# One transfer in place of four for the inverse of a unit, and one in place of three for the 80-row part of a stack

## The chip, the cores and the metric

The kernel runs on one core of one Trainium2 chip. The metric is device time in microseconds of one execution; the number that counts is the median of the runs.

## What is computed

The first part is a linear recurrence over 768 time steps for 4 batches of 8 heads (each state is 40 x 40):

```python
for t in range(S):
    y[:, :, t] = einsum('bhd,bhde->bhe', rt, state)
    Sa = einsum('bhde,bhe->bhd', state, at)
    state = state * wt[:, :, None, :] - einsum('bhd,bhe->bhde', Sa, bt) + einsum('bhd,bhe->bhde', vt, kt)
```

Its output, laid out as 3072 rows of 320, goes through a mixture of experts: noisy top-2 routing over 8 experts, `relu(x @ w1[e]) @ w2[e]` for the rows of each expert, weighted and summed.

## The kernel before

The recurrence is done in chunks of 64 time steps. Two pairs of batches (`p` = 0, 1) and 12 chunks give 24 units, numbered `n` = 0 to 23 in the order of their work. Four units (two chunks of both pairs) make a group `g` = 0 to 5. Within a unit the recurrence becomes matrix products with the inverse of a unit triangular matrix, which is built from 32 x 32 diagonal blocks: four blocks (`i` = 0 to 3) for each of 8 heads.

Preparation of a group, for each `p` (`prepA`, `scoresL`, `prepC`):

- VectorE takes running products of `w` (L495) and scales `b` (L518), `a` (L520) and `k` (L544) by them; ScalarE and VectorE split each into two half-precision parts, `pk` (L459, L460). `b` and `a` go to a buffer in HBM called `d_ab` (stores at L519 for `b`, L521 for `a`), `k` to `d_k` (L547). The input tiles `rawba` and `rawk` exist once, so the next load of each (L491, L538) waits until the split of the last one has read it.
- A stack `st_ab` of 120 rows is read back from `d_ab`: rows 40 to 119 with three transfers, one for each `gg` (L524), rows 0 to 39 with two, one for each of `a` and `b` (L525).
- TensorE multiplies `a` with `b` from the stack (`psc<-st_ab`), ScalarE copies the results to `lt` and `lo` (L556), and four transfers put the 32 x 32 blocks into `scr` in HBM (L558).
- `tsolve` loads `scr` as `X` with one matrix in each of 128 partitions (L563), masks it (L564), inverts by 30 steps of a multiply (L570) and an add (L571), and stores the result to `scr2` (L573). Groups 0 and 1 do this on VectorE, groups 2 to 5 on GpSimd (`TPOOL`).

A unit (`chain`, `outp`): `fetchA` loads `Vz`, `vu`, `st_k`, `RV` (L580, L581, L478, L585), `fetchB` loads the inverse `T` from `scr2` two units ahead, with four transfers of 32 partitions (L593). `apply` multiplies with `T` (`pQ<-w,T`), twice in a unit. The output row block is `xt` (L691), stored at L95, and routed a few units at a time.

All these transfers but GpSimd's own are issued from one queue, SyncE's (SP in the profile), which is in order: where one transfer waits for its data or its buffer, all behind it wait. A scheduler of the build sets the order on every engine, from priorities in the code (`high_priority`) and its own estimate of times; the estimate changes with the number of transfers, so the written order of the code doesn't fix the order of the program. Engines run their own instructions in order too. After the units, eight experts follow (`hidden` at L287, `output` at L309); their weights are loaded at L224, L225 and L229, those of the first expert while the last units run.

Of the kernel before, what the change touches and what calls it, by code (L numbers as in the profile page):

```python
# [8 lines left out]
F32 = mybir.dt.float32  # L9
# [354 lines left out]
NP,NG,CG,C=2,6,2,64  # L364
# [39 lines left out]
class Att:  # L404
# [81 lines left out]
    def prepA(s,p,g):  # L486
        nc=s.nc; FM=s.aps[0]; V=Behind(s.tc,nc.vector,s.tl) if g==1 else nc.vector
        sh=[120,NS,64]; W0=NS*65
        w=s.inp.tile([120,W0],F32,name="raww",bufs=2); nc.sync.dma_start(w,FM[p,g][:,:W0])
        ba=s.inp.tile([120,2*X],F32,name="rawba",bufs=BAB)  # L490
        for i in range(2): nc.sync.dma_start(ba[:,X*i:X*i+X],FM[p,g][:,W0+X*i:W0+X*i+X])  # L491
        b_,a_=ba[:,:X],ba[:,X:]
        Gx=s.tmp.tile([120,NS,65],F32,name="Gx")
        fl=lambda z: z.rearrange("p a b->p (a b)")
        V.tensor_tensor_scan(fl(Gx),w,fl(s.d1),0.0,op0=ALU.mult,op1=ALU.add)  # L495
        P=Gx[:,:,1:65]
        r0=w[:,:X].rearrange("p (a b)->p a b",a=NS)
        nc.scalar.activation(r0,P,AF.Ln)
        nc.scalar.activation(r0,r0,AF.Exp,scale=-1.0)
        NH=s.tmp.tile(sh,F32,name="NH",bufs=2)  # L500
        V.tensor_tensor(NH,P,r0,op=ALU.mult)
        nr=r0
        V.scalar_tensor_tensor(nr,NH,2.0,r0,op0=ALU.subtract,op1=ALU.mult)
        V.tensor_tensor(NH,nr,P[:,:,31:32].to_broadcast(sh),op=ALU.mult)
        NG_=s.late.tile(sh,F32,name="NG_",bufs=NGB)
        s.pl=(V if g in MG else nc.gpsimd).tensor_tensor(NG_,Gx[:,:,0:64],nr[:,:,31:32].to_broadcast(sh),op=ALU.mult)
        nge=s.tmp.tile([120,CG+1,3,2],F32,name=f"nge{p}",bufs=2)
        v4=lambda z: z.rearrange("p (a c b) t->p c a b t",a=3,c=CG)
        if g==0: V.memset(nge[:,0],0.0)
        else: V.tensor_copy(nge[:,0],s.nge[p][:,CG])  # L510
        V.tensor_tensor(nge[:,1:CG+1],v4(Gx)[:,:,:,:,64],v4(nr)[:,:,:,:,31],op=ALU.mult)
        s.nge[p]=nge
        gm=s.tmp.tile([120,2,3,CG],F32,name="gm")
        V.tensor_tensor(gm.rearrange("p b a c->p c a b"),nge[:,0:CG],v4(Gx)[:,:,:,:,32],op=ALU.mult)
        G={'p':p,'g':g,'NH':NH,'ng':NG_.rearrange("p (a c b) t->p a c (b t)",a=3,c=CG),'gm':gm}
        d=s.dr.tile([2,120,2,X],F16,name="d_ab",bufs=2)
        dv=d.rearrange("l p x n->p l x n")
        (V if g in MD else nc.gpsimd).tensor_tensor(b_,b_,fl(NH),op=ALU.mult)  # L518
        s.pack(b_,-SC,1,1,V=V,out=lambda pk: nc.sync.dma_start(dv[:,:,1],pk))  # L519
        (V if g in MD else nc.gpsimd).tensor_tensor(a_,a_,fl(NG_),op=ALU.mult)  # L520
        s.pack(a_,-SC,0,1,V=V,out=lambda pk: nc.sync.dma_start(dv[:,:,0],pk))  # L521
        st=s.sab[(2*g+p)%SAB].tile([120,18*K],F16,name="st_ab")
        sv=st.rearrange("p (g x n)->p g x n",g=3,x=2); dv=d.rearrange("l (e g) x n->(l e) g x n",g=3)
        for gg in range(3): nc.sync.dma_start(sv[40:120,gg],dv[:,gg])  # L524
        for x in range(2): s.sd0=nc.sync.dma_start(sv[0:40,:,x],dv[40*x:40*x+40,:,x])  # L525
        for i,z in enumerate('ab'): G[z]=[s.operand(st,2,i,CG,c) for c in range(CG)]
        pg=s.ps.tile([128,3,3*CG],F32,name="pg",tag="pp",bufs=s.PPB)
        for gg in range(3):
            for b in range(2):
                nc.tensor.matmul(pg[64*b:64*b+64,gg],s.selg[:,gg],gm[:,b].rearrange("p a c->p (a c)"),start=True,stop=True)  # L530
        gv=s.gam[p][:,:,g*CG:(g+1)*CG]
        V.tensor_copy(gv,pg.rearrange("p q (a c)->p (q a) c",a=3))
        return G
# [15 lines left out]
    def scoresL(s,G,gi,scr):  # L549

        nc=s.nc
        lt=s.tmp.tile([128,CG,8,32],F32,name="lt",bufs=LTB)
        lo=s.late.tile([128,CG,8,32],F32,name="lo",bufs=LOB)
        for c in range(CG):
            pp=s.score64(G['b'][c],G['a'][c],"pp",s.PPB)
            for z,t0 in ((lt,0),(lo,32)): nc.scalar.activation(z[:,c],pp[:,:,t0:t0+32],AF.Copy,scale=-(2.0**-18))  # L556
        for i in range(4):
            s.sl=s.nc.sync.dma_start(scr[gi,i].rearrange("c h (j t)->j (c h) t",j=32),(lt,lo)[i%2][32*i:32*i+32].rearrange("p c h t->p (c h) t"))  # L558
        G['lo']=lo
    def tsolve(s,scr,eng):  # L560
        nc=s.nc
        Xt=s.tmp.tile([128,32,32],F32,name="X",bufs=2)
        s.xd=s.nc.sync.dma_start(Xt.rearrange("p a b->p (a b)"),scr.rearrange("g i c h x->(g i c h) x"))  # L563
        eng.tensor_tensor(Xt,Xt,s.tri,op=ALU.mult)  # L564
        eng.memset(Xt.rearrange("p a b->p (a b)")[:,0:1024:33],1.0)
        T=s.tmp.tile([128,240],F32,name="Tt")
        for j in range(1,31):
            m=31-j
            t=T[:,:j*m].rearrange("p (k i)->p k i",i=m)
            eng.tensor_tensor(t,Xt[:,j:j+1,j+1:].to_broadcast([128,j,m]),Xt[:,0:j,j:j+1].to_broadcast([128,j,m]),op=ALU.mult)  # L570
            s.tl=eng.tensor_tensor(Xt[:,0:j,j+1:],Xt[:,0:j,j+1:],t,op=ALU.add)  # L571
        scr2=s.dr.tile([2,4,CG,8,32,32],F32,name="scr2")
        (nc.gpsimd if eng is nc.gpsimd else nc.sync).dma_start(scr2.rearrange("g i c h j x->(g i c h) (j x)"),Xt.rearrange("p j t->p (j t)"))  # L573
        return scr2

    def fetchA(s,G,cc,c,n):
# [12 lines left out]
        return o  # L589
    def fetchB(s,o,scr2,n):  # L590
        nc=s.nc; G,c=o['G'],o['c']; p=G['p']; T=s.Ts[n]=s.stk.tile([128,8,32],F32,name="T",bufs=TB)
        for i in range(4):
            s.nc.sync.dma_start(T[32*i:32*i+32],scr2[p,i,c].rearrange("h j x->j h x"))  # L593
    def warm(s,src,k):
        if not k: return
        for _ in range(k): s.nc.tensor.matmul(src,s.idh,s.dm[:,0:320],start=True,stop=True)
# [96 lines left out]
    def run(s,m,xo=None):  # L693
        nc=s.nc
        grp={}; scr={}; scr2={}; O={}
        N=NG*4
        def prepA(g,p):
            if p==0: grp[g]=[]; scr[g]=s.dr.tile([2,4,CG,8,1024],F32,name="scr")
            with s.tc.high_priority(offset=PA_):
                G=s.prepA(p,g); grp[g].append(G); s.scoresL(G,p,scr[g])  # L700
        def prepT(g):
# [3 lines left out]
        def idx(n): g,q=divmod(n,4); c,p=divmod(q,2); return g,c,p,g*CG+c  # L705
# [4 lines left out]
        def fB(n):  # L710
            if n<N: s.fetchB(O_(n),scr2[idx(n)[0]],n)
        after=s.tc.issue_after
        prepA(0,0); prepA(0,1); pl=s.pl.ins; prepT(0); xd,tl=s.xd.ins,s.tl.ins
        gate=(s.sd0,s.sl)
        s.prepC(grp[0][0],gate)
# [4 lines left out]
        with after(xd),(after(tl) if TG else ExitStack()):  # L720
            prepA(1,0); prepA(1,1); prepT(1)
# [3 lines left out]
        for n in range(N):  # L725
            g,c,p,cc=idx(n); ga,qa=divmod(n+LA,4); gc,qc=divmod(n+LC,4)
            if ga>1 and ga<NG and qa<2:
                with (after(s.sd0.ins) if n<=GA else ExitStack()): prepA(ga,qa)
                if qa: prepT(ga)
            if 0<gc<NG and qc<2:  # L730
                with (after(s.sd0.ins) if n<=GC else ExitStack()): prepC(gc,qc)
            with s.tc.high_priority(offset=PRIO):
                sD=s.chain(p,cc,O[n])
            fB(n+2)
            if n+1<N: s.pre(O[n+1])
            xt=s.wk.tile([128,360],F32,name="xt",bufs=2)
            s.outp(O[n],sD,xt); xt=xt[:,0:DM]
            if n+1<N: s.blocks(O[n+1])
            fA(n+2)
            if m is not None:  # L740
                m.drain(1); m.logits(2*cc+p,xt,s.ps,("pt","pp"),(s.PT,s.PPB))
                if ZN<=n<ZN+4:
                    with after(m.xw.ins): m.zero(n-ZN)
            else: nc.sync.dma_start(xo[p,cc],xt)
# [153 lines left out]
```

## Time and profile before

| | us |
|---|---|
| median of 3 runs (1033.17 to 1034.09) | 1033.28 |
| the profiled execution | 1035.52 |
| its span, first to last instruction | 1033.7 |
| busy TensorE, VectorE, ScalarE, GpSimd | 814.5, 554.3, 391.0, 321.1 |
| share of the chain that ended last: TensorE, VectorE, DMA, SP's queue | 53%, 21%, 14%, 3% |

The profile is of one execution, 2.2 us above the median. Busy times are shares of the span; the chain that ended last is followed back from the last instruction, at each step to what released it. A view by windows gives each engine's busy time in a stretch, the TensorE clock granted there (1.00 is 2.4 GHz, 0.50 is 1.2 GHz) and the mean busy share of the 16 DMA engines.

### The profile page before, as it was taken

What the parts mean: (1) busy time and instruction counts of PE and PEld (TensorE: products, weight loads), DVE (VectorE), ACT (ScalarE), POOL (GpSimd) and SP (SyncE); (2) the same over time, 40 slices, a digit from 0 to 9 for tenths busy, and PEclk for the clock granted to TensorE, in tenths of its full rate; (3) what the DMA queues carried; (4) which work ended last, traced back from release to release, by engine and by line L of the source; (5) the groups of instructions that cost most, each with busy time, mean ns of one, the idle gap of its engine ahead of it and who ended that gap; (6) DMA issues with size and microseconds to landing.
All of it is one profiled execution on the core that took longest, in us unless ns stands there. A gap on an engine that the chain in (4) does not pass through costs nothing.

```text
span 1033.7 us, 27409 instructions
## 1 busy us (share of the span) xinstructions
PE 814.5 (79%) x11706; PEld 712.2 (69%) x11706; DVE 554.3 (54%) x1198; ACT 391.0 (38%) x820; POOL 321.1 (31%) x456
## 2 busy tenths in 40 slices
PE   0114558669857876998896789999999999999994
PEld 0113446557746755877775668898989898989994
DVE  9268667944757666338554762643434444443420
ACT  2203443334633542454443432543434444443420
POOL 5000000393077039209401005316060606060312
PEclk9999986558967976998997699999999999999997
DMA  4785896593784684473486403516161616161302
GB/s 121 183 231 127 214 266 151 146 239 102 163 247 156 139 209 112 116 173 121 127 256 203 126 8 73 163 24 167 28 154 43 159 37 157 38 148 49 36 8 37
DMA packets 127111, 135.89 MB, mean 131 GB/s; under 512 B 59248, under 2 KB 106804, under 8 KB 126900
## 3 DMA queue, kind: packets, MB, share of 16 engines
q1 hardware_dynamic: 116292, 114.90, 41.5%
q0 software_dynamic: 10688, 19.14, 9.7%
q8 instruction: 94, 1.54, 0.6%
q14 instruction: 37, 0.30, 0.1%
HBM read 96.25 MB, written 41.03 MB: 133 GB/s over the span
## 4 chain that ended last, share of the span: by engine, by line
PE 53%; DVE 21%; DMA 14%; issue 4%; ACT 4%; SPq 3%; POOL 0%; POOLq 0%; DVEq 0%; ACTq 0%
PE po L309 17%; PE ph L287 15%; DMA rawk<-in_fm_dram 6%; PE psc L470 4%; PE pY L470 3%; DMA d_ab<-pk 2%; PE pW L470 2%; PE pQ L470 2%; PE pt L268 2%; DVE X L571 2%; DVE Tt L570 2%; DVE w2l L244 1%; DVE pk L460 1%; PE pst L470 1%; DVE ohB L162 1%
## 5 line engine op out<-in xcount | busy, mean ns | idle before, releaser
L311 POOL DMA_INDIRECT out_dram<-y,oi x56 | 92.3, 1648 | 236.9 <-ACT y L310 212.1
L290 DVE SCALAR_TENSOR_TENSOR hl<-ph,hh 128x256 fp32r<-128x256 f32 (+1 forms) x128 | 70.1, 554 | 120.5 <-ACT hh L288 111.3
L288 ACT ACTIVATE hh<-ph 128x320 fp32r<-128x320 f32 (+1 forms) x128 | 64.7, 518 | 147.6 <-PE ph L287 141.5
L564 POOL TENSOR_TENSOR X<-X,tri 128x1024 f32<-128x1024 f32 x4 | 9.0, 2242 | 309.2 <-DVE ak L606 179.3
L309 PE MATMUL po<-w2h,hh 128*128 128x320 f32 x384 | 75.4, 314 | 5.0 <-DVE y L304 3.9
L470 PE MATMUL psc<-RV,uT 128*64 128x128 f32 x384 | 63.0, 317 | 17.0 <-DVE P L680 15.1
L571 POOL TENSOR_TENSOR X<-X,Tt 128x30 f32<-128x30 f32 (+14 forms) x120 | 72.2, 602 | 8.7
L570 POOL TENSOR_TENSOR Tt<-X 128x30 f32<-128x30 f32 (+14 forms) x120 | 70.1, 584 | 8.4
L309 PE MATMUL po<-w2h,hl 128*128 128x320 f32 x384 | 70.8, 311 | 0.0
L287 PE MATMUL ph<-xh,w1h 128*128 128x512 f32 (+1 forms) x256 | 69.7, 355 | 1.0 <-DVE hl L290 1.0
L470 PEld LDWEIGHTS psc<-RV,uT 128*64 128x64 f32 x384 | 50.0, 160 | 27.6 <-DVE P L680 16.5
L287 PE MATMUL ph<-xh,w1l 128*128 128x512 f32 (+1 forms) x256 | 68.9, 350 | 0.0
L287 PE MATMUL ph<-xl,w1h 128*128 128x512 f32 (+1 forms) x256 | 68.6, 349 | 0.0
L252 POOL DMA_INDIRECT xr<-xd,gi x56 | 53.7, 959 | 47.6 <-issue 14.3
L309 PEld LDWEIGHTS po<-w2h,hh 128*128 128x128 f32 x384 | 61.0, 188 | 9.9 <-issue 5.0
L309 PE MATMUL po<-w2l,hh 128*128 128x320 f32 x384 | 65.7, 309 | 0.0
L470 PE MATMUL pQ<-w,T 32*32 32x40 f32 x2304 | 46.7, 224 | 23.7 <-DMA T<-scr 23.1
L680 DVE TENSOR_TENSOR P<-psc,mk 128x512 f32<-128x512 f32 x48 | 32.9, 686 | 59.3 <-PE psc L470 59.1
L470 PEld LDWEIGHTS pQ<-w,T 32*32 32x32 f32 x2304 | 39.6, 128 | 36.3 <-issue 32.1
L470 PE MATMUL psc<-RV 128*64 128x128 f32 x384 | 63.1, 317 | 0.0
L309 PEld LDWEIGHTS po<-w2h,hl 128*128 128x128 f32 x384 | 59.8, 188 | 0.5
L309 PEld LDWEIGHTS po<-w2l,hh 128*128 128x128 f32 x384 | 58.6, 188 | 0.1
(312 smaller groups left out, 1883.7 us busy)
## 6 DMA issues: line engine op xcount, KB each, us to landing
w2r<-in_w_dram SPq DMA_DIRECT2D x8, 1280.0 KB
RV<-in_rv_dram SPq DMA_DIRECT2D x48, 192.0 KB
rawba<-in_fm_dram SPq DMA_DIRECT2D x24, 360.0 KB
d_ab<-pk SPq DMA_DIRECT2D x24, 360.0 KB
st_ab<-d_ab SPq DMA_DIRECT2D x36, 240.0 KB
w1r<-in_w_dram SPq DMA_DIRECT2D x8, 1024.0 KB
raww<-in_fm_dram SPq DMA_DIRECT2D x12, 365.6 KB
st_ab<-d_ab SPq DMA_DIRECT2D x24, 180.0 KB
```

What stands on the lines that cost most here:

```text
L162: nc.vector.tensor_tensor(B[:,j],D[:,j].rearrange("p k (o m)->p k o m",o=1).to_broadcast([128,2,4,64]),vl[:,j].rearrange("p k (f o)->p k f ...
L252: k=t//128; nc.gpsimd.indirect_dma_start(out=X[:p,k if s.cap==CAP else 0],out_offset=None,in_=s.xd[int(w is not s.early[0])],in_offset=OFF ...
L268: for t,p in tiles(t0,n): nc.tensor.transpose(pt[:,t-t0:t-t0+p],x[:p,t//128,f0:f0+128],s.idm[:p,:p])
L287: for i,(a,b) in enumerate(mm): nc.tensor.matmul(ph[:,:n],a,b,start=i==0,stop=i==7)
L288: nc.scalar.activation(hh[:,f,:n],ph[:,:n],AF.Relu)
L290: if c.stop>c.start: nc.vector.scalar_tensor_tensor(o,ph[:,c],0.0,hh[:,f,c].bitcast(F32),op0=ALU.max,op1=ALU.subtract)
L309: s.lm=nc.tensor.matmul(po[:p],h[:,f,r],w[:,f],start=k==0,stop=k==23); k+=1
L311: st=nc.gpsimd.indirect_dma_start(out=s.out_d,out_offset=OFFS(ap=idx[:p,e,ii:ii+1],axis=0),in_=y[:p],in_offset=None,compute_op=ALU.add)
L470: def mm(s,*a,**k): return lambda: s.nc.tensor.matmul(*a,**k)
L570: eng.tensor_tensor(t,Xt[:,j:j+1,j+1:].to_broadcast([128,j,m]),Xt[:,0:j,j:j+1].to_broadcast([128,j,m]),op=ALU.mult)
L571: s.tl=eng.tensor_tensor(Xt[:,0:j,j+1:],Xt[:,0:j,j+1:],t,op=ALU.add)
L680: nc.vector.tensor_tensor(m,pp.rearrange("p i j t->p (i j) t"),s.mk.to_broadcast([128,8,64]),op=ALU.mult)
```

## The change

- `scr` and `scr2` keep their matrices in the order chunk, head, block in place of block, chunk, head (the block index `i` goes behind `c` and `h`). The stores of L558 write the same runs of 32 numbers to other places; the load and the store of `tsolve` stay one transfer each, with the matrices of the 128 partitions in the new order.
- With that order the rows `(i j)` of a unit's inverse lie at one stride, and `fetchB` loads all 128 partitions with one transfer in place of four. There are 24 units: 72 transfers fewer.
- The 80-row part of a stack is loaded with one transfer in place of three. There are 12 stacks: 24 transfers fewer.

No arithmetic changes. Lines after L593 are one lower in the changed kernel, and `T` is loaded at its L592.

```diff
-        for gg in range(3): nc.sync.dma_start(sv[40:120,gg],dv[:,gg])
+        nc.sync.dma_start(sv[40:120].rearrange("p g x n->p (g x n)"),dv.rearrange("p g x n->p (g x n)"))
...
-            s.sl=s.nc.sync.dma_start(scr[gi,i].rearrange("c h (j t)->j (c h) t",j=32),(lt,lo)[i%2][32*i:32*i+32].rearrange("p c h t->p (c h) t"))
+            s.sl=s.nc.sync.dma_start(scr[gi,:,:,i].rearrange("c h (j t)->j (c h) t",j=32),(lt,lo)[i%2][32*i:32*i+32].rearrange("p c h t->p (c h) t"))
...
-        s.xd=s.nc.sync.dma_start(Xt.rearrange("p a b->p (a b)"),scr.rearrange("g i c h x->(g i c h) x"))
+        s.xd=s.nc.sync.dma_start(Xt.rearrange("p a b->p (a b)"),scr.rearrange("g c h i x->(g c h i) x"))
...
-        scr2=s.dr.tile([2,4,CG,8,32,32],F32,name="scr2")
-        (nc.gpsimd if eng is nc.gpsimd else nc.sync).dma_start(scr2.rearrange("g i c h j x->(g i c h) (j x)"),Xt.rearrange("p j t->p (j t)"))
+        scr2=s.dr.tile([2,CG,8,4,32,32],F32,name="scr2")
+        (nc.gpsimd if eng is nc.gpsimd else nc.sync).dma_start(scr2.rearrange("g c h i j x->(g c h i) (j x)"),Xt.rearrange("p j t->p (j t)"))
...
-        for i in range(4):
-            s.nc.sync.dma_start(T[32*i:32*i+32],scr2[p,i,c].rearrange("h j x->j h x"))
+        s.nc.sync.dma_start(T,scr2[p,c].rearrange("h i j x->(i j) h x"))
...
-            if p==0: grp[g]=[]; scr[g]=s.dr.tile([2,4,CG,8,1024],F32,name="scr")
+            if p==0: grp[g]=[]; scr[g]=s.dr.tile([2,CG,8,4,1024],F32,name="scr")
```

The build's scheduler answers with another order of SP's queue and of the engines between the first unit and about the fourth; behind that the orders are nearly the same but for the merged transfers. Three places of SP's queue follow. The name of a tile is followed by the number of its buffer where the listing has one.

The first place is SP's queue where the stack of group 1, `p` = 1, is written and read (the stores of its `b` and its `a` half are L519 and L521; the 40-row reads at L525 need one half each). Before:

```order
L489 DMA raww<-in_fm_dram 120x780
L519 DMA d_ab<-pk 120x2x768
L521 DMA d_ab<-pk 120x2x768
L525 DMA st_ab<-d_ab 40x3x768
L491 DMA rawba<-in_fm_dram 120x768 x2
L524 DMA st_ab<-d_ab 80x1536 x3
L525 DMA st_ab<-d_ab 40x3x768
L547 DMA d_k<-pk 120x4x384
```

And in the changed kernel:

```order
L489 DMA raww<-in_fm_dram 120x780
L519 DMA d_ab<-pk 120x2x768
L525 DMA st_ab<-d_ab 40x3x768
L521 DMA d_ab<-pk 120x2x768
L491 DMA rawba<-in_fm_dram 120x768
L558 DMA scr<-lt 32x16x32
L558 DMA scr<-lo 32x16x32
L558 DMA scr<-lt 32x16x32
L524 DMA st_ab<-d_ab 80x4608
L525 DMA st_ab<-d_ab 40x3x768
L558 DMA scr<-lo 32x16x32
L547 DMA d_k<-pk 120x4x384
```

The store of the `a` half (L521) now stands behind the first 40-row read (L525), which waits for the `b` half to have landed, and three block stores of `p` = 0 stand ahead of the 80-row read.

The second place is SP's queue where the stack of group 2, `p` = 1, is read, the `k` of group 2 is stored (L547) and the next `k` is loaded (L538). Before:

```order
L524 DMA st_ab<-d_ab 80x1536 x3
L558 DMA scr<-lt 32x16x32
L585 DMA RV_175<-in_rv_dram 48x1024 x2
L558 DMA scr<-lo 32x16x32
L558 DMA scr<-lt 32x16x32
L558 DMA scr<-lo 32x16x32
L525 DMA st_ab<-d_ab 40x3x768
L547 DMA d_k<-pk 120x4x384
L538 DMA rawk<-in_fm_dram 120x768
```

And in the changed kernel:

```order
L524 DMA st_ab<-d_ab 80x4608
L585 DMA RV_175<-in_rv_dram 48x1024 x2
L525 DMA st_ab<-d_ab 40x3x768
L547 DMA d_k<-pk 120x4x384
L538 DMA rawk<-in_fm_dram 120x768
L519 DMA d_ab<-pk 120x2x768
L558 DMA scr<-lt 32x16x32
L558 DMA scr<-lo 32x16x32
L558 DMA scr<-lt 32x16x32
L558 DMA scr<-lo 32x16x32
```

The store and the load of `k` now stand ahead of the four block stores.

The third place is SP's queue behind the end of group 1's `tsolve`, where the inverses of units 4 to 7 are loaded. Before:

```order
L573 DMA scr_782<-X 128x1024
L489 DMA raww<-in_fm_dram 120x780
L95 DMA xd_839<-xt 128x320
L593 DMA T<-scr_782 32x8x32 x12
L580 DMA Vz_172<-in_vt_dram 64x320 x2
L547 DMA d_k<-pk 120x4x384
L593 DMA T<-scr_782 32x8x32 x4
L521 DMA d_ab<-pk 120x2x768
L491 DMA rawba<-in_fm_dram 120x768 x2
L538 DMA rawk<-in_fm_dram 120x768
```

And in the changed kernel, from the second pair of inverses on:

```order
L592 DMA T<-scr_768 128x8x32 x2
L581 DMA vu<-in_vt_dram 64x2x320
L558 DMA scr<-lt 32x16x32
L558 DMA scr<-lo 32x16x32
L558 DMA scr<-lt 32x16x32
L558 DMA scr<-lo 32x16x32
L580 DMA Vz_172<-in_vt_dram 64x320 x2
L563 DMA X<-scr 128x1024
L521 DMA d_ab<-pk 120x2x768
L491 DMA rawba<-in_fm_dram 120x768 x2
L547 DMA d_k<-pk 120x4x384
L538 DMA rawk<-in_fm_dram 120x768
```

The load of `k` (L538) now follows its store (L547) at once; no load of an inverse stands between them or ahead of `rawba`.

## Rows read from the trace of the kernel before

**Rows 1.** Windows by stage: units 0 to 3, the other units, the experts.
```profile
core 0: us, PE busy (x) PEld busy (x) DVE busy (x) ACT busy (x) POOL busy (x), PEclk, DMA share, GB/s
85.00:235.00 150.00, 95.44 (x1792) 79.99 (x1793) 108.52 (x192) 55.28 (x114) 35.62 (x47) 0.76 0.76 195
235.00:602.00 367.00, 300.36 (x7257) 248.16 (x7257) 216.65 (x507) 156.78 (x377) 127.65 (x236) 0.84 0.59 158
602.00:1033.70 431.70, 409.78 (x2488) 376.52 (x2486) 174.79 (x378) 163.65 (x305) 142.59 (x111) 0.99 0.35 80
```
**Rows 2.** The chain that ended last, 200 to 240: start, us, what.
```profile
209.74 8.32 DMA rawk<-in_fm_dram
...
218.12 7.05 DMA d_ab<-pk
...
227.50 5.14 DMA rawk<-in_fm_dram
```
**Rows 3.** VectorE's timeline: start, us, what, [idle before it, and its releaser].
```profile
149.24 1.23 DVE L564 TENSOR_TENSOR X<-X,tri 128x1024 f32<-128x1024 f32 x1 [1.82 <-DMA X<-scr]
...
172.36 1.02 DVE L544 TENSOR_TENSOR rawk<-rawk,NH 120x384 f32<-120x384 f32 x2 [6.45 <-DMA rawk<-in_fm_dram]
...
201.77 1.04 DVE L460 SCALAR_TENSOR_TENSOR pk<-rawk,pk 120x768 f16<-120x768 f32 x1
...
213.03 1.06 DVE L518 TENSOR_TENSOR rawba<-rawba,NH 120x768 f32<-120x768 f32 x1 [5.52 <-DMA rawba<-in_fm_dram]
...
218.08 1.43 DVE L544 TENSOR_TENSOR rawk<-rawk,NH 120x384 f32<-120x384 f32 x2 [1.21 <-DMA rawk<-in_fm_dram]
```
**Rows 4.** Line L593, the loads of `T`: nanoseconds min/median/max of an issue.
```profile
L593 SPq DMA_DIRECT2D T<-scr x96: 308/448/1803, 85.5 to 520.6; - x96
```
**Rows 5.** Windows: unit 0's start, the stretch after it, the first expert's weights.
```profile
85.00:95.00 10.00, 4.99 (x132) 4.27 (x134) 8.70 (x13) 3.51 (x6) 0.00 (x0) 1.00 0.42 77
95.00:165.00 70.00, 42.77 (x816) 35.91 (x810) 51.28 (x88) 30.67 (x61) 0.00 (x0) 0.90 0.92 235
520.00:560.00 40.00, 32.65 (x721) 25.74 (x707) 24.11 (x86) 13.86 (x37) 5.11 (x9) 0.85 0.88 256
```
**Rows 6.** SP's timeline at the third place: start, us, what.
```profile
196.94 5.75 SPq L593 DMA_DIRECT2D T<-scr  x12
...
204.02 0.54 SPq L547 DMA_DIRECT2D d_k<-pk  x1
204.61 3.08 SPq L593 DMA_DIRECT2D T<-scr  x4
...
209.74 0.48 SPq L538 DMA_DIRECT2D rawk<-in_fm_dram  x1
```
**Rows 7.** SP's timeline at the second place.
```profile
158.88 1.28 SPq L585 DMA_DIRECT2D RV<-in_rv_dram  x2
...
164.76 0.84 SPq L547 DMA_DIRECT2D d_k<-pk  x1
```
**Rows 8.** SP's timeline at the first place.
```profile
108.51 0.33 SPq L521 DMA_DIRECT2D d_ab<-pk  x1
112.43 0.78 SPq L525 DMA_DIRECT2D st_ab<-d_ab  x1
...
114.31 1.27 SPq L524 DMA_DIRECT2D st_ab<-d_ab  x3
```
**Rows 9.** SP's timeline at the loads for units 20 to 23.
```profile
507.10 4.61 SPq L593 DMA_DIRECT2D T<-scr  x8
511.81 2.07 SPq L580 DMA_DIRECT2D Vz<-in_vt_dram  x2
```
**Rows 10.** TensorE's timeline: scores of group 1; unit 20's first use of `st_k`.
```profile
124.77 0.64 PE L470 MATMUL psc<-st_ab 120*64 120x64 f16 x16 [4.38 <-DMA RV<-in_rv_dram]
...
526.89 0.43 PE L470 MATMUL psc<-st_ab,st_k 120*64 120x64 f16 x16
```

## The prediction

> **What bounds the kernel now.** I read the windows by stage first. The experts (the last 432 us) keep TensorE busy for 410 of 432 us at the full clock [rows 1], and the change touches nothing there. Units 4 to 23 take 367 us with TensorE busy for 300. The weak stretch is 85 to 235, units 0 to 3: TensorE is busy for 95 of 150 us at a granted clock of 0.76, VectorE for 109 [rows 1]. Then the chain of waits. In that stretch it runs through transfers that feed the preparation of the next groups: a load of `rawk` of 8.32 us, a store of `d_ab` of 7.05, the next `rawk` of 5.14 [rows 2]. Last VectorE's timeline: it is in order, carries both the preparation and the units, and stands still for 6.45 us at 172.36 and 5.52 us at 213.03 because a loaded input has not landed [rows 3]. TensorE's next matmuls wait behind it. So what counts is when SP's queue issues `rawk` and `rawba`, and the loads of `T` are worth something only where they stand ahead of those.
>
> The profiled execution took 1035.5 us, 2.2 us above the median. The sum is made against it and the same difference taken from the median.
>
> **The change part by part.** 96 issues go. One load of `T` takes 0.448 us to issue [rows 4]. A load of 128 partitions isn't in the trace: its issue lies between one of the shortest, 0.308, and four medians, 1.79. I take 0.45, because the queue's other issues stand near that whatever their shape: 0.54 for `d_k`, 0.48 for `rawk` [rows 6]. Then 72 loads of `T` and 24 of stacks are 43 us of SP's queue, but nearly all of it lies beside other work. The bytes and the short runs of `T` stay as they are, so its time on the DMA engines stays. The moves inside `scr` and `scr2` change only addresses: nothing, covered by the same transfers as before; if the new strides cost the block stores something, it would show as a later `X`.
>
> *Units 0 to 3's inverses (85 to 93).* Sixteen issues become four. VectorE is busy for 8.70 of the 10 us [rows 5], so what SP issues behind them isn't wanted sooner, and unit 0 needs all four parts either way. Nothing; the cover is VectorE's work, and without it the gain would be at most the 12 issues, 5.4 us.
>
> *Third place, units 4 to 7's inverses.* Before, VectorE finishes the split of `k` at 202.81 [rows 3], `d_k` is issued at 204.02 and over at 204.56, and then four loads of `T` (3.08 us), the store of `a` and two loads of `rawba` stand ahead of `rawk`, issued at 209.74 [rows 6]. In the new order `rawba` comes ahead of `d_k` and `rawk` right behind it. The earlier twelve loads of `T` shrink from 5.75 us to under 2, so `rawba` finds the queue free. `rawk` can go at 204.6: 5.1 us sooner. VectorE's waits that follow, 5.52 us for `rawba` and 1.21 for `rawk` [rows 3], are all of this kind, and the store and the next `rawk` of the chain [rows 2] follow from them. Bounds: nothing, if the transfer lands no sooner, and 6.7 us, both waits. I take 5.1, near the upper end, because the chain passes through just these issues. Late next is the split of `a` and `b` on ScalarE and VectorE.
>
> *Second place.* Before, the second `d_k` of group 2 is issued at 164.76, 4.6 us behind the end of `RV` (158.88 + 1.28 = 160.16) [rows 7]; between them stand three block stores that wait for ScalarE, and one stack read. In the new order only the stack read, 0.78 us as at 112.43 [rows 8], remains: `d_k` and `rawk` go 3.8 us sooner. VectorE waits 6.45 us for that `rawk` in the middle of `tsolve`, and 1.82 us at its start for `X` [rows 3], which moves ahead of three stack reads too. Bounds: nothing, and 8.3 us with both waits gone. I take 3.8, what the issue gains. What moves back, the four block stores, only has to reach GpSimd's `tsolve` of group 2, whose inverse isn't used before unit 8. From 95 to 165 the DMA engines are busy to 0.92 [rows 5], so there is little room for more.
>
> *First place.* The store of the `a` half waits for the `b` half to land: it moves from 108.51 to behind 112.43 + 0.78 = 113.21, 4.7 us later [rows 8]. The stack read at 114.31 waits for it; the read itself shrinks from 1.27 us to about 0.45, so the stack is some 3.9 us later. TensorE already waits 4.38 us for it at 124.77 [rows 10]. I count nothing, because the scores behind it are copied by ScalarE ahead of a split that stood in their way before, so `X` isn't later for it; if that cover is gone, 3.9 us (rival B).
>
> *Weights of the first expert.* They move ahead of unit 20's `st_k`, `RV` and unit 23's `T`. With three loads of `T` and two of `Vz` behind 507.10 [rows 9], the weights are issued from about 507.1 + 3 x 0.45 + 2.07 = 510.5. They are 2.9 MB by the shapes in the code; at the 256 GB/s of 520 to 560 [rows 5] they take 11.3 us, to 521.8. Unit 20's `st_k` is first used at 526.89 [rows 10]: 5 us of cover, so nothing; at 180 GB/s they would take 16 us and end there, and each us more would cost one.
>
> Sum: 5.1 + 3.8 = 8.9 us. The profiled execution would take 1035.5 - 8.9 = 1026.6, the median **1033.3 - 8.9 = 1024.4 us**.
>
> **The rivals.** The bound of a measurement here is about 0.2%, 2 us, so 1031.2 to 1035.4 is no change.
>
> A. *The DMA engines are the bound, not the queue: no change.* For it: a share of 0.92 from 95 to 165 [rows 5], with the same bytes to move. An issue that goes sooner then only waits in another place, `rawk` lands at 172 as before, and what is won at 204 is lost in the same way. Against it: at 85 to 95 the share is 0.42 [rows 5], and the load at 209.74 follows SP's issue at once. It gives 1033.3. The Trainium skill, DMA: Bandwidth & Descriptors, in "Issuing engines are not separate DMA queues", says that what is saved on a sequencer's issue time is usually small relative to the transfer itself; by that rule the sum would be near nothing. The trace agrees for most of the 96 issues, and not for those on the chain [rows 6].
>
> B. *The `a` half's store is caught behind a wait: slower.* The stack of group 1, `p` = 1, is 3.9 us later, TensorE stands at its scores in order with unit 1's second half behind them, `X` and VectorE's `tsolve` follow, and the full DMA engines take away the gains. It decides if the scores start later than 124.77 + 2, and `X` is masked later than 149.24. 1033.3 + 3.9 = 1037.2 us.
>
> C. *The merge doesn't do what it says:* the new strides might split the 128-partition load so that it fills one queue for four issues, 1.79 us. Then the third place would keep 3 x (0.448) of its 5.1 and the gain would be 7.6: still faster, at 1025.7.
>
> **How the numbers follow.** The forecast with C, faster by over 0.2%: 0.63. A: 0.16. B, and with it orders that the scheduler made worse where I haven't looked: 0.21. The lower end takes both upper bounds, 6.7 + 8.3 = 15.0, and 2 us more for a clock in units 0 to 3 that rises as waits go (0.76 now, 0.84 later [rows 1]): 1016. The upper end is B: 1037.5. Beyond lie fewer than 2 in 10.
>
> **What would show it.** In the profile after: 24 loads of `T` in L592 with an issue near 0.45 us; `rawk` issued under 1 us behind its `d_k` after VectorE's `tsolve`; VectorE's wait for `rawk` inside `tsolve` down from 6.45 us by about 4, and for `rawba` behind it near nothing; the window of units 0 to 3 about 9 us shorter, the experts' window unchanged. I am wrong if `rawk` lands as late as before although issued sooner (A), if the scores of group 1 start at 127 or later and `X` behind them (B), or if units 19 to 21 stand waiting for `st_k`.

## The result and the profile after

| | before | after |
|---|---|---|
| median of 4 runs each, one chip (us) | 1033.55 (1033.17 to 1034.09) | 1043.17 (1041.18 to 1047.09) |
| ratio, 95% interval | | 1.0103 [1.0067, 1.0139] |
| profiled execution / its span (us) | 1035.52 / 1033.7 | 1041.5 / 1039.8 |

The change makes the kernel 1% slower. I had forecast 1024.4, faster, with an upper end of 1037.5: the sign was wrong.

The windows by stage after the change, to be held against [rows 1, 5] (same columns):

```profile
core 0: us, PE busy (x) PEld busy (x) DVE busy (x) ACT busy (x) POOL busy (x), PEclk, DMA share, GB/s
85.00:95.00 10.00, 4.58 (x144) 4.20 (x144) 8.28 (x16) 4.56 (x7) 0.00 (x0) 1.00 0.60 118
85.00:235.00 150.00, 92.54 (x1873) 77.35 (x1873) 105.96 (x195) 56.03 (x116) 24.28 (x37) 0.80 0.77 196
```

VectorE is busy for 106 of the 150 us where it was busy for 109, and TensorE for 93 instead of 95: the weak stretch is as weak as before. The issue of the merged load went as assumed; this is its line (ns min/median/max), against [rows 4]:

```profile
L592 SPq DMA_DIRECT2D T<-scr x24: 383/474/2312, 86.2 to 517.3; - x24
```

SP's queue at the second place, against [rows 7] (start, us, what):

```profile
157.54 1.46 SPq L585 DMA_DIRECT2D RV<-in_rv_dram  x2
159.05 0.81 SPq L525 DMA_DIRECT2D st_ab<-d_ab  x1
159.90 0.51 SPq L547 DMA_DIRECT2D d_k<-pk  x1
160.46 0.47 SPq L538 DMA_DIRECT2D rawk<-in_fm_dram  x1
```

`d_k` goes at 159.90 in place of 164.76, 4.9 us sooner; I had counted 3.8. At the third place, against [rows 6]:

```profile
196.10 2.81 SPq L581 DMA_DIRECT2D vu<-in_vt_dram  x1
199.00 0.55 SPq L558 DMA_DIRECT2D scr<-lt  x1
...
202.71 0.35 SPq L563 DMA_DIRECT2D X<-scr  x1
203.15 0.39 SPq L489 DMA_DIRECT2D raww<-in_fm_dram  x1
203.59 0.38 SPq L95 DMA_DIRECT2D xd<-xt  x1
204.03 0.43 SPq L521 DMA_DIRECT2D d_ab<-pk  x1
204.50 1.75 SPq L491 DMA_DIRECT2D rawba<-in_fm_dram  x2
206.35 1.01 SPq L547 DMA_DIRECT2D d_k<-pk  x1
207.40 0.63 SPq L538 DMA_DIRECT2D rawk<-in_fm_dram  x1
```

`rawk` stands directly behind `d_k`, as the listing said, but goes at 207.40, 2.3 us sooner than 209.74 and not 5.1. `rawba` didn't find the queue free. From 196.10 on SP issues, with no pause above 0.3 us, what the new order puts ahead of it: a load of `vu` whose issue alone lasts 2.81 us (why was not followed), four block stores, `Vz`, `X`, `raww`, an `xd` store and the store of `a` (the listing of the third place lacks `raww` and `xd`). VectorE's split of `a` had ended at 202.39, 1.6 us before its store was issued, so the queue and not the split set the time of `rawba`. VectorE's own timeline has changed too (idle before, and its releaser, in brackets), against [rows 3]:

```profile
169.46 1.03 DVE L544 TENSOR_TENSOR rawk<-rawk,NH 120x384 f32<-120x384 f32 x2 [3.22 <-DMA rawk<-in_fm_dram]
172.04 0.48 DVE L690 TENSOR_TENSOR xt<-pY,xt 128x320 f32<-128x320 f32 x1
...
190.46 0.69 DVE L679 TENSOR_TENSOR P<-psc,mk 128x512 f32<-128x512 f32 x1 [1.93 <-PE psc L470]
...
194.61 0.69 DVE L605 TENSOR_TENSOR ak<-psc,mk 128x512 f32<-128x512 f32 x1 [1.69 <-PE psc L470]
197.23 0.96 DVE L506 TENSOR_TENSOR NG__2455<-Gx,raww 120x768 f32<-120x768 f32 x1 [1.92 <-PE pgm L471]
198.10 0.48 DVE L690 TENSOR_TENSOR xt<-pY,xt 128x320 f32<-128x320 f32 x1
...
202.78 0.95 DVE L460 SCALAR_TENSOR_TENSOR pk<-rawk,pk 120x768 f16<-120x768 f32 x1
...
212.78 0.96 DVE L518 TENSOR_TENSOR rawba<-rawba,NH 120x768 f32<-120x768 f32 x1 [4.91 <-DMA rawba<-in_fm_dram]
...
216.71 1.71 DVE L544 TENSOR_TENSOR rawk<-rawk,NH 120x384 f32<-120x384 f32 x2 [2.68 <-DMA rawk<-in_fm_dram]
```

And the end of unit 1 on VectorE before, which the prediction never looked at:

```profile
159.80 0.48 DVE L691 TENSOR_TENSOR xt<-pY,xt 128x320 f32<-128x320 f32 x1
```

The last step of unit 1 (`xt`) has moved from 159.80 to 172.04. The scheduler has put pieces of group 1's `tsolve` ahead of it on VectorE: 25 of its 60 steps in place of 9. With `tsolve` used up earlier (its store goes at 188.55, before at 193.81), VectorE has nothing to fill the gaps of units 2 and 3, and waits for TensorE at 190.46, 194.61 and 197.23. The split of `k`, which ended at 202.81 before, now starts at 202.78, behind unit 2's `xt`. The wait for `rawk` inside `tsolve` fell from 6.45 to 3.22 us. But up to the end of unit 3 VectorE's waits for `rawba` and `rawk` add to 19.5 us after and 17.6 before, and its waits for TensorE to 5.5 and 0.5: nothing was won in sum.

Where the time goes over all units is best read on one chip: three profiled executions there, the end of `xt` of a unit by VectorE's timeline (start plus duration), in us. The third kernel, explained below, merges `T` alone and keeps the order of before.

| end of unit | 1 | 3 | 7 | 18 | 19 | 21 | 23 | span |
|---|---|---|---|---|---|---|---|---|
| before (f1) | 159.7 | 226.4 | 306.6 | 512.2 | 526.4 | 575.3 | 603.2 | 1028.4 |
| after (f2) | 171.9 | 226.3 | 308.3 | 510.4 | 530.7 | 570.2 | 608.0 | 1034.6 |
| `T` merged, order of before (f3) | 159.1 | 220.6 | 298.7 | 506.9 | 521.2 | 564.8 | 592.6 | 1018.2 |

After the change, unit 3 ends when it did before; unit 7 is 1.7 us late; unit 19 loses 6 us, which come back by unit 21; units 22 and 23 take 37.8 us in place of 27.9. The experts take 425.2 us before and 426.6 after. On most chips executions of one kernel scatter by over 1%, so single profiles show places, and the ratios below show what a place costs.

### The profile page after: what moved, and what is told of

Its sections match the earlier page's. It is cut to its first block, busy times and chain, and to the rows that moved or that the text cites. A ratio compares the mean times of both kernels' runs of the same rounds, so it can differ in the third digit from the quotient of the medians.

```text
span 1039.8 us, 27317 instructions
## 1 busy us (share of the span) xinstructions
PE 814.2 (78%) x11706; PEld 713.9 (69%) x11706; DVE 554.7 (53%) x1198; ACT 391.4 (38%) x820; POOL 320.3 (31%) x456
## 4 chain that ended last, share of the span: by engine, by line
PE 59%; DVE 16%; DMA 14%; issue 4%; ACT 3%; SPq 3%; POOL 0%; POOLq 0%; DVEq 0%; ACTq 0%
PE ph L287 18%; PE po L309 16%; DMA rawk<-in_fm_dram 6%; PE psc L470 4%; PE pY L470 4%; PE pQ L470 2%; DMA d_ab<-pk 2%; PE pW L470 2%; PE pt L268 2%; DMA rawba<-in_fm_dram 2%; DVE X L571 1%; DVE Tt L570 1%; PE pu L471 1%; PE pS L470 1%; PE pst L470 1%
## 5 line engine op out<-in xcount | busy, mean ns | idle before, releaser
L470 PE MATMUL psc<-RV,uT 128*64 128x128 f32 x384 | 65.9, 327 | 30.3 <-DVE P L679 26.2
L470 PE MATMUL psc<-RV 128*64 128x128 f32 x384 | 66.0, 327 | 0.0
```

What stands on the lines that cost most here:

```text
L470: def mm(s,*a,**k): return lambda: s.nc.tensor.matmul(*a,**k)
```

## The experiments

The theory: merging `T` gains about what I forecast, but the changed number of transfers made the build's scheduler draw another order for all engines, and this order costs more than that. The rivals: the merged transfers themselves cost time (they land later, or delay others); the new addresses in `scr` and `scr2` cost; or the cost lies at one place, such as the first expert's weights.

The two orders differ a good deal. With the loads of `T` and of a stack counted as one each, 125 of 441 places on SP, 235 of 1175 on VectorE, 102 of 821 on ScalarE and 1062 of 8243 on TensorE hold another instruction; GpSimd's are the same. Most lie between 85 and 240 us; of VectorE's, 63 lie between 510 and 600, none in the experts. The order behind the fourth unit is thus less alike than the section on the change has it. To hold an order fixed, most kernels below add this to the end of the build: for each engine a chain of order-only edges, no wait and no work, after a table of the wanted order.

```diff
+def pin(nc,tc,table):
...
+        for a,b in zip(run,run[1:]):
+            tc.add_manual_dep(b,a.name,mybir.DependencyInfo(mybir.DependencyClass.NoSync,mybir.DependencyReason.DATA),reason="pin")
...
         build(nc, tc, aps, out)
+        pin(nc, tc, TABLE)
```

What differs from kernel to kernel is then the loads and the table; orders in pieces are cut by the time at which an instruction stands in the profile of before. Ratios are to the kernel before on the same chip, with 95% intervals. No run holds a kernel to its own order alone; the nearest is g3 below, held to before's order and at 1.0026.

**The order against the merges.** e1: the changed kernel, table of before's order. e2: the kernel before with its seven loads, table of after's order.

```diff
 e1: the changed kernel
+        pin(nc, tc, TABLE)
 e2: the kernel before
+        pin(nc, tc, TABLE)
```

> The changed transfers (one load of T, one stack load) with every engine's instructions pinned to the order of the kernel before. Theory O, the order: what was lost came with the order that the build's scheduler made of the new transfer count, so here it is gone: 1029 to 1034 us, with unit 7, unit 19 and units 22 to 23 as long as before (28.8, 14.3 and 27.8 us). Theory X, the transfers: a merged load lands later (T 3.65 us in the middle against 2.48 for a quarter, the stack part 7.41 against 5.92), and what waits for it starts later whatever the order: 1041 us or more.

> The reverse: the kernel before, with its four loads of T and three stack loads, pinned on every engine to the order of the changed kernel. Theory O: as slow as the changed kernel or slower, since 96 issues come back into the same order: 1041 to 1050 us. Theory X: the transfers are the old ones, so 1031 to 1035 us.

e1 measured 0.9913 [0.9879, 0.9948], e2 1.0125 [1.0072, 1.0179]. With the order held, both merges together are faster; with the old loads, the new order alone is slower. That is the theory's sign on both sides, and it rules out that the merged transfers are what costs.

**Which stretch of the order.** e3: both merges, after's order to 510 us and before's behind; e4 the reverse.

```diff
 e3, e4: the changed kernel
+        pin(nc, tc, TABLE)
```

> The changed kernel in its own order up to unit 18 (510 us) and in the order of before behind that. In the two profiles unit 18 ends 1.1 us later after the change, unit 23 ends 11.6 us later, and the experts are 5.5 us shorter. If the order behind 510 us makes the loss (O, tail): 1033.5 + 1.1 = 1034.6 us, less if the shorter experts have another cause. If the order before 510 us makes it (O, head), or the transfers (X): 1041 us or more.

> The complement: the changed transfers, the order of before up to 510 us, and the order of the changed kernel behind it (weights of expert 0 ahead of the loads of unit 20; the splits of the weights ahead of unit 22's work on VectorE). O, tail: 10.4 us lost in units 19 to 23, up to 5.5 given back by the experts: 1038 to 1044 us. O, head: 1031 to 1035. X: 1041 or more, as in the first of these runs.

e3 0.998 [0.9941, 1.0019], e4 0.9985 [0.9947, 1.0023]. Each half takes back about 0.7% of what e1 has; neither alone makes the change slower.

**The two merges apart, with controls.** f1 is the kernel before, f2 the changed kernel, both under new names. f3 and its repeat n0 merge `T` alone, g3 the stack alone, all three in before's order; g0 repeats e1.

```diff
 f3, n0: three loads of a stack put back
-        nc.sync.dma_start(sv[40:120].rearrange("p g x n->p (g x n)"),dv.rearrange("p g x n->p (g x n)"))
+        for gg in range(3): nc.sync.dma_start(sv[40:120,gg],dv[:,gg])
...
 g3: the kernel before, one load of a stack
-        for gg in range(3): nc.sync.dma_start(sv[40:120,gg],dv[:,gg])
+        nc.sync.dma_start(sv[40:120].rearrange("p g x n->p (g x n)"),dv.rearrange("p g x n->p (g x n)"))
```

> The kernel before, unchanged, as a run of its own on this chip, for its trace beside those of the pinned kernels. Every theory: a ratio of 1.000 within 0.004.

> The changed kernel, unchanged. If the two halves of the order simply add to the merged transfers in the order of before (0.9913 + 0.0067 + 0.0072 from the pinned runs), the ratio is 1.005; if they hinder each other, 1.010 as first measured.

> The merge of T alone, with three stack loads, pinned to the order of before. If what counts is the number of issues on SP's queue (72 of the 96 that go), three quarters of the 8.7 thousandths that both merges gained in that order: a ratio of 0.9935. If the stack load is what counts (it stands on the way to the scores): 0.998 or more. If all comes from T: 0.991.

> The merge of T alone in the order of before, once more. If the first run holds: 0.989. If the stack load makes no difference and chips scatter: the mean of this run's kin (0.989, 0.991, 0.997), 0.992 to 0.994.

> The stack merge alone, with four loads of T, in the order of before. If it costs what lies between the runs of T alone (0.989) and of both (0.991 and 0.997): 1.002 to 1.008. If it is worth its 24 issues (a quarter of the gain): 0.997. If nothing: 1.000.

> Both merges in the order of before, once more, on the chip of the runs that follow. By its first run 0.991; by the merge of T alone (0.989) plus a stack load that costs or gains nothing, 0.989 to 0.991. Above 0.995 the first run was chance.

f1 0.9988 [0.9957, 1.002]; f2 1.0107 [1.0061, 1.0153], the first result again, and above the 1.005 that the halves of the order would give if they added. f3 **0.9886** [0.9856, 0.9917] (1020.06 us) and n0 **0.9937** [0.9903, 0.997] (1026.69): merging `T` gains 0.6 to 1.1%, in the mean 0.9%. That this is the 8.9 of 1033 us that I forecast for the whole change is partly luck: 3.8 of those were for moves at the second place, which f3 and n0 don't have. g3 1.0026 [0.9989, 1.0063]: the stack's merge gains nothing that can be measured. g0 0.9972 [0.9937, 1.0006] gains less than e1, and by its own expectation (above 0.995) e1's 0.9913 was partly chance; the mean of the two, 0.994, lies between f3 and n0 plus g3.

At the third place the mechanism is the forecast one: the issues of `T` hold up the loads behind them. SP's queue of f3 at the third place (start, us, what), against [rows 6]:

```profile
193.30 1.72 SPq L592 DMA_DIRECT2D T<-scr  x3
...
198.84 0.36 SPq L547 DMA_DIRECT2D d_k<-pk  x1
199.25 0.45 SPq L592 DMA_DIRECT2D T<-scr  x1
...
201.31 1.18 SPq L491 DMA_DIRECT2D rawba<-in_fm_dram  x2
202.54 1.29 SPq L538 DMA_DIRECT2D rawk<-in_fm_dram  x1
```

and of f1, the kernel before on the same chip:

```profile
195.42 5.75 SPq L593 DMA_DIRECT2D T<-scr  x12
...
202.50 0.54 SPq L547 DMA_DIRECT2D d_k<-pk  x1
203.10 2.71 SPq L593 DMA_DIRECT2D T<-scr  x4
...
206.35 1.47 SPq L491 DMA_DIRECT2D rawba<-in_fm_dram  x2
207.86 0.45 SPq L538 DMA_DIRECT2D rawk<-in_fm_dram  x1
```

Twelve issues of 5.75 us became three of 1.72, four of 2.71 one of 0.45, and `rawk` goes at 202.54 in place of 207.86, 5.3 us sooner. Of these, 1.7 us were there before the place: VectorE's split of `k` ended at 198.82 in f3 and at 200.55 in f1. The other 3.6 are the queue's: in f1 it was still issuing `T` and `Vz` when the split was done. VectorE's waits for `rawba` and `rawk` from 85 us to the end of unit 7 add to 26.8 us in f1 (ten of them) and to 18.8 in f3 (seven). The difference, 8.0 us, is what unit 7 ends sooner in the table above, 7.9. The wait behind the third place, f3:

```profile
206.85 1.33 DVE L518 TENSOR_TENSOR rawba<-rawba,NH 120x768 f32<-120x768 f32 x1 [3.32 <-DMA rawba<-in_fm_dram]
```

and f1:

```profile
211.17 1.32 DVE L518 TENSOR_TENSOR rawba<-rawba,NH 120x768 f32<-120x768 f32 x1 [5.92 <-DMA rawba<-in_fm_dram]
```

The traces of the other runs show the same place. In the seven profiles with `T` merged and before's order up to 510 us (f3, n0, e1, g0, k1, k2, e4) unit 3, in which the third place lies, takes 28.5 to 30.0 us from the end of unit 2 to its own; in the four with four loads of `T` in before's order (before, f1, p2, g3) it takes 32.6 to 33.7.

f3, `T` merged in before's order, is the best version of this study and beats both kernels.

**The addresses, and another order.** p2: the new layout of `scr` and `scr2` with all seven loads, which leaves the order as it was. p1: new layout and `T` merged, the stack in three loads, no table: the scheduler decides.

```diff
 p2: the kernel before with the new layout
-            s.nc.sync.dma_start(T[32*i:32*i+32],scr2[p,i,c].rearrange("h j x->j h x"))
+            s.nc.sync.dma_start(T[32*i:32*i+32],scr2[p,c,:,i].rearrange("h j x->j h x"))
...
 p1: the same layout
-        for i in range(4):
-            s.nc.sync.dma_start(T[32*i:32*i+32],scr2[p,i,c].rearrange("h j x->j h x"))
+        s.nc.sync.dma_start(T,scr2[p,c].rearrange("h i j x->(i j) h x"))
```

> The new addresses in scr and scr2 alone, with four loads of T and three stack loads; the scheduler's order is that of before without a pin. The prediction counted nothing for the addresses: 1.000 within 0.004. If the strides of 512 KB blocks cost the stores or the loads of X something, or help them: 1.004 or more, or 0.996 or less, and then part of the gain of T's merge is theirs.

> The merge of T alone, in the order that the build's scheduler makes of it (a third order: 307 of VectorE's 1175 places and 172 of SP's 441 differ from before). Pinned to the order of before it gave 0.989 and 0.994. If the order decides more than the merge, this lies anywhere from 0.98 to 1.02 and away from 0.991 by over 0.004; if the merge alone is what counts and only the stack load led the scheduler astray: 0.989 to 0.994.

p2 0.9993 [0.9946, 1.004]: the addresses cost nothing that can be measured. p1 **1.0198** [1.0152, 1.0244]: the same instructions as f3 and n0, in a third order (172 of 441 places differ from before on SP, 307 of 1175 on VectorE), are 2% slower than before where f3 is 1.1% faster. It loses mostly in units 7 to 10; unit 3 ends at 228.0 (p2 229.1), unit 7 at 314.7 (307.3), unit 10 at 383.9 (364.8), unit 23 at 625.5 (605.3). The windows about units 7 to 10, p1:

```profile
284.00:384.00 100.00, 69.72 (x1574) 57.67 (x1574) 59.98 (x136) 37.06 (x88) 38.95 (x72) 0.76 0.68 167
```

and p2:

```profile
280.00:365.00 85.00, 65.69 (x1582) 54.40 (x1576) 59.53 (x136) 36.95 (x88) 39.18 (x72) 0.80 0.66 179
```

The same work of VectorE, ScalarE and GpSimd takes 100 us in place of 85, and TensorE is idle for 30 us in place of 19. Which instruction holds it up there wasn't followed.

**Which places of the order.** All with both merges: f4 takes after's order to 136 us only, g1 from 136 to 240, k1 from 510 to 560 (the weights), k2 from 560 on (the splits of the first expert's weights); all else is before's. m1 takes SP's order of after to 240 us and leaves all other engines in before's; m2 the reverse.

```diff
 f4, g1, k1, k2, m1, m2: the changed kernel
+        pin(nc, tc, TABLE)
```

> Both merges, the order of the changed kernel up to 136 us (the prediction's first place, where the store of the a half stands behind the b half's landing), and the order of before behind it. Rival B of the prediction: this place costs 3.9 us, a ratio of 0.995 against 0.9913 for the order of before throughout. If the loss of the first half of the order lies in the later places: 0.991. If all of it lies here: 0.998.

> Both merges, the order of the changed kernel from 136 to 240 us (the prediction's second and third place, units 1 to 3), the order of before elsewhere. The prediction counted 8.9 us for the moves in these places. If the moves bring that on top of the merges: 0.983. If the merges alone bring it and the moves are worth nothing: 0.991, as with the order of before. If this is where the first half of the order loses (the first half cost 0.0067, the first place alone 0.0039 of it): 0.994 or more.

> Both merges, the order of the changed kernel from 510 to 560 us alone: expert 0's weights ahead of unit 20's stack and RV loads and unit 23's T. The profile of the changed kernel shows unit 19 as 6.0 us longer and units 20 and 21 as 9.3 us shorter than before on the same chip. If the delay stays (the prediction: each us past the cover costs one): 0.997. If it is given back because the weights are then out of the way of units 20 and 21: 0.990 to 0.992.

> Both merges, the order of the changed kernel from 560 us on alone: six splits of expert 0's weights on VectorE, put ahead of unit 21's and 22's own work. Units 22 and 23 take 37.8 us in the changed kernel against 27.9 before, on the same chip, with a granted clock of 0.5 through most of it. If that is the order's doing: 9.9 us, a ratio of 1.000 against 0.991. If it came from the late loads before it: 0.991.

> Both merges; SP's queue up to 240 us in the order of the changed kernel (all three places of the prediction), the other engines, and SP behind that, in the order of before. The prediction: these moves are what gains, 8.9 us: 0.985. If the merges gain by themselves and the moves of SP are worth nothing: 0.991 to 0.997. If the moves of SP make the loss of the first half: 1.001 or more.

> The reverse: both merges; VectorE, ScalarE and TensorE up to 240 us in the order of the changed kernel, SP in the order of before throughout. If the order of the engines makes the loss (VectorE's tsolve of units 4 to 7 ahead of unit 1, which leaves nothing to fill units 2 and 3): 1.001 or more. If SP's order makes it: 0.991 to 0.997.

f4 0.9952 [0.9926, 0.9978]: no loss that shows against both merges in before's order (0.994, from other chips), but 0.7% above f3 on the same chip, which lacks only the stack's merge. In its profile VectorE waits 7.25 us for `rawba` at 144.40, which f3 doesn't, and unit 3 ends at 225.1 in place of 220.6. As with g1, the cut has a part in that: behind 136 us VectorE is back in before's order. What the first place costs by itself, nothing or up to 0.7%, stays open.

g1 1.0067 [1.0029, 1.0105]: against g0, on the same chip, the order of 136 to 240 costs some 1%. It holds one wait that the changed kernel lacks, since without the first place's moves `X` comes later:

```profile
148.70 1.23 DVE L564 TENSOR_TENSOR X<-X,tri 128x1024 f32<-128x1024 f32 x1 [9.53 <-DMA X<-scr]
```

In the changed kernel that wait is 2.45 us at 141.74. So the order of 136 to 240 relies on the order ahead of it, and g1 overstates its price; e3, which has both, lost 0.7%.

k1 0.9957 [0.9926, 0.9988] and k2 0.9963 [0.9935, 0.999], against 0.9972 for g0 on the same chip: neither costs anything that shows. Yet all profiles with after's order behind 560 us (after, f2, e2, e4, k2) take 35.5 to 38.2 us for units 22 and 23, all others 27.3 to 27.9, and e4, both stretches together, lost 0.7% against e1. Whether the end of the order costs nothing or up to 0.7% stays open.

m1 **1.0105** [1.0048, 1.0162]: the very moves of SP's queue that I counted as a gain of 8.9 us lose 1% against the kernel before, and 1.6% against both merges in before's order (0.994), when the engines keep their order. VectorE of m1:

```profile
129.60 0.96 DVE L520 TENSOR_TENSOR rawba<-rawba,NG__1091 120x768 f32<-120x768 f32 x1 [9.97 <-DMA rawba<-in_fm_dram]
148.32 0.96 DVE L518 TENSOR_TENSOR rawba<-rawba,NH 120x768 f32<-120x768 f32 x1 [7.31 <-DMA rawba<-in_fm_dram]
...
222.72 1.14 DVE L518 TENSOR_TENSOR rawba<-rawba,NH 120x768 f32<-120x768 f32 x1 [11.22 <-DMA rawba<-in_fm_dram]
```

Its waits for `rawba` alone add to 40.2 us up to unit 7; in n0, on the same chip, to 4.4. The reason for the first is in SP's queue of m1 at the first place:

```profile
113.39 0.42 SPq L491 DMA_DIRECT2D rawba<-in_fm_dram  x1
...
119.62 2.29 SPq L585 DMA_DIRECT2D RV<-in_rv_dram  x2
121.96 0.43 SPq L538 DMA_DIRECT2D rawk<-in_fm_dram  x1
122.43 0.44 SPq L491 DMA_DIRECT2D rawba<-in_fm_dram  x1
```

Before, both loads of `rawba` went together (f1: 113.11, two in 0.94 us). Now the second goes at 122.43, behind the block stores, `RV` and `rawk`. m2 loses as well, 1.0167 [1.0114, 1.022]; its waits were not followed here. The order of a queue and that of the engines belong together.

## Why the prediction was wrong

By its steps:

- **Issue of a merged load**, 0.45 us: right, 0.474 in the median, and rival C (a load that fills the queue) is out: the four issues of `T` at the third place take 0.40 to 0.58 us each.
- **First inverses, addresses, stack merge**, nothing each: right within the noise. VectorE is busy for 8.28 of the first 10 us, p2 gives 0.9993, g3 1.0026.
- **Third place, 5.1 us: the step that failed.** "`rawba` finds the queue free" and "`rawk` can go at 204.6" take SP's new order with the engines' old times, and leave out what the new order puts ahead of `rawba`: from `vu` to the store of `a`, 8.4 us of issues from 196.10 to 204.46. `rawba` went at 204.50, `rawk` 2.3 us sooner (0.9 in f2 against f1), and the wait for `rawba` was 4.91 us in place of 5.52 (2.04 and 5.92 on the other chip), not "near nothing". VectorE's order is new as well: `tsolve` of units 4 to 7 ahead of unit 1, the preparation behind unit 2. So the waits for `rawba` and `rawk` up to the end of unit 3, which the sum lets fall by 8.9 us, stayed: 17.6 before, 19.5 after, 15.7 in f1, 16.3 in f2. In before's order, with nothing new ahead of `rawba`, they fall to 8.5 (f3) and 9.3 (n0).
- **Second place, 3.8 us**: right for the queue (4.9 us) and nearly for the wait (6.45 to 3.22 us), but the units paid: unit 1 ended 12.2 us later, and by the end of unit 3 all of it was gone (226.3 against 226.4 on one chip). The 6.45 itself, the upper bound's main part, scatters: the same wait is 3.73 us in f1, 5.58 in p2 and 2.01 in g3, and f2's is 2.54.
- **First place, nothing**: in the changed kernel the stack's delay cost nothing that shows, and it was the wrong term to weigh. The 4.38 us of [rows 10] are put down there to a load of `RV`; I read them as a wait for the stack. The scores start at 125.20, before 126.8, and `X` is masked at 141.74, before 149.24: rival B's condition did not occur. What I overlooked is the second load of `rawba`, which moves 9 us back; alone with before's engines it is a wait of 9.97 us (m1). With after's order of VectorE throughout it is covered: the waits are 0.56 and 0.64 us there. Cut off at 136 us (f4) it is not.
- **Weights, nothing**: the cover was misread. I took unit 20's first use of `st_k` from the scores at 526.89 [rows 10]; it is read before that, by `ptr`, so the cover was 0.2 us and not 5. TensorE before (start, us, what):

```profile
522.02 0.36 PE L470 MATMUL ptr<-cmb,st_k 120*128 120x40 f16 x8
```

  and after:

```profile
525.77 0.32 PE L470 MATMUL psc<-RV,uT 128*64 128x128 f32 x1 [2.35 <-issue]
...
526.99 0.47 PE L470 MATMUL ptr<-cmb,st_k 120*128 120x40 f16 x8
```

  The loads, by SP's queue of after:

```profile
510.56 0.52 SPq L224 DMA_DIRECT2D w1r<-in_w_dram  x1
...
513.19 1.62 SPq L478 DMA_DIRECT2D st_k<-d_k  x2
514.91 0.78 SPq L585 DMA_DIRECT2D RV<-in_rv_dram  x2
```

  Unit 19 takes some 6 us more, but not as "units 19 to 21 stand waiting for `st_k`" had it: `ptr` follows without a pause. TensorE stops for 2.35 us (2.63 in f2) at 525.77, in the middle of a run of matmuls, at one that waits for no semaphore; the profile names no releaser ("issue"), and the cause stays open. The DMA engines are busy to 1.00 in unit 19 there and to 0.75 before, and the granted clock of the unit is 0.77 in place of 1.00. By unit 21 it is made up in f2; in k1's profile it is not, though k1's ratio shows no lasting cost.
- **What wasn't in the sum at all**: units 22 and 23, where the splits of the first expert's weights now stand ahead of unit work on VectorE. The windows of units 22 and 23, before and after (columns as above):

```profile
575.00:602.00 27.00, 23.20 (x444) 19.44 (x443) 14.89 (x54) 8.64 (x25) 0.65 (x3) 0.81 0.36 118
575.00:613.50 38.50, 30.44 (x443) 25.00 (x444) 19.88 (x60) 10.95 (x28) 0.65 (x3) 0.58 0.27 85
```

  The same matmuls take 30.4 us of TensorE in place of 23.2, at a granted clock of 0.58 in place of 0.81 (0.50, 1.2 GHz, from 581 to 613; before, the clock was at 0.50 from 570 to 580 and at 1.00 from 590 on), and TensorE is idle for 8.1 us in place of 3.8. What this costs in the end is not settled (k2, e4).

- **Rival A** (the DMA engines bound it): not so in before's order, where loads issued sooner took 8.0 us off VectorE's waits (f1 to f3). The Trainium skill, DMA: Bandwidth & Descriptors, "Issuing engines are not separate DMA queues", holds that the sequencer's time to start a transfer is usually small beside the transfer. The stack's merge (1.0026) agrees, where that saving is all there is; the gain of `T`'s (0.9886 and 0.9937) has another source, that its issues stood ahead of other loads on the chain of waits.
- **The outcome** came by what I had put into rival B as "orders that the scheduler made worse where I haven't looked", with a share of 0.21 and no price. e2 prices the order at 1.25%, 13 us: larger than the whole gain. With the merges in it, that order takes 1.0103 and 1.0107, so in it the 96 issues were worth 0.2%, nothing within the intervals: the merge's gain is shown in before's order alone. The parts do not add exactly: 0.991 (`T`) + 0.0026 (stack) + 0.0125 (order) is 1.006, measured is 1.0103 and 1.0107; the missing 0.4% is within the intervals and unassigned.

Shown by runs: the merge of `T` gains 0.6 to 1.1% in before's order, and the redrawn order costs more. Read from profiles only: that within the order it is the early `tsolve` that starves units 2 and 3, and that units 22 and 23 take 10 us more; no kernel moved the `tsolve` alone, and k2, which moved the end alone, shows no cost in its ratio. Not tried: a table that takes after's good moves (the second place) without VectorE's.

## What to carry to other kernels

Where a scheduler sets the order, a merged transfer is two changes: the transfer, and a new draw of the order on every engine, which here was worth 1 to 3%, more than the merge. Read the new order on the engines that wait, not only on the queue that was edited, and don't combine a queue's new order with an engine's old times. Measure the edit with the order held before judging it, and if it gains, keep that order.

## What the runs showed that I had not expected

- The same instructions in two orders took 0.9886 and 0.9937 (before's), and 1.0198 (the scheduler's own for the `T` merge) of the time before: a span of some 3% without a change in work.
- The issue time of a load of 128 partitions (0.474 us in the median) is nearly that of 32 (0.448), so a merge of four saves three whole issues.
- The unchanged kernel's median differs from job to job, each on one chip: 1030.8, 1033.6, 1034.3, 1036.0, 1037.5 and 1042.9 us in the six jobs. That is as much as the effect under study; only ratios on one chip can be compared.
